# Attention and two dense stages on one core: PSUM banks as tiles of their own, and another order of products, copies and conversions

## The chip, the cores and the metric

The kernel runs on one core of a Trainium2 chip. The metric is the device time of one execution in microseconds (us), less is better. Five engines work side by side, each through its own queue in program order: TensorE (PE; PEld is its loading of weights), VectorE (DVE), ScalarE (ACT), GpSimd (POOL) and SyncE (SP), which here issues most of the DMAs. Results of TensorE land in PSUM, eight banks of 512 fp32 per partition; ACT and DVE read them there.

## The reference

The outputs of an attention with a soft cap (2 x 12 heads, 448 positions, head size 64) form 896 rows of 768, which go through two dense stages, 768 to 2048 to 768 each, the first with h * cos(h), the second with Silu:

```python
scores = cap * np.tanh(scale * np.matmul(q, k.transpose(0, 1, 3, 2)) / cap)
attn = np.exp(scores - np.max(scores, axis=-1, keepdims=True))
x = np.matmul(attn / (np.sum(attn, axis=-1, keepdims=True) + 1e-09), v)
x = np.ascontiguousarray(x.transpose(0, 2, 1, 3)).reshape(B * S, H * D)
h = x @ w_in1;  x = (h * np.cos(h)) @ w_out1
h = x @ w_in2;  return (h * (1.0 / (1.0 + np.exp(-h)))) @ w_out2
```

## The kernel before

Each fp32 operand is split into a high and a low part, and a product is made of three passes of matmuls: high with high, high with low, low with high. The weights come as 64-bit numbers: `w_load` brings a block (two buffers, `wraw`), `w_abs` (ACT) and the three steps of `w_bits` (DVE) turn it into fp32, `w_hi` (ACT) and `w_lo` (DVE) split it into two of the tiles of `room`. The program order of every engine is written out by hand (`manual_schedule`): an engine does its instructions in the order in which the code emits them, and waits where one is not ready.

The stages are attention, `gemm_in` (first weight of the first stage, with cos), `gemm_out` (second weight; result y), `gemm_sums` (first weight of the second stage, with Silu) and `gemm_last` (its second weight). `mm3` (L472) holds the matmuls of `gemm_in` and `gemm_out`, `prod` (L725) those of `gemm_sums`, L898 is `gemm_last`.

`gemm_out` makes six column blocks dm of y^T, each for the two batches b of 448 columns, in three cuts of k. Each block and batch is a sum in one bank. Cut n of block dm also converts the weight that is three cuts ahead, then, in block 5, the first pair of weights of `gemm_sums` (`first_pair`). `gemm_sums` multiplies blocks of 2 x 2 with seven products in place of eight (the scheme of Strassen and Winograd). Its right sides come from y: B11, T1 from blocks 0 to 2 (`y_low`), and B21, B22, T2, T3, T4 from blocks 3 to 5 (`y_high`), each with a high and a low part (`split_hi` on ACT, `split_lo` on DVE). `kept["f"]` is a scratch tile of two halves.

`gemm_sums` runs over eight pairs p of weight blocks. The left sides of a pair are A, S31, S24 and A22; `s31` and `s24` (DVE) form the sums, `take` (ACT) the high and `low` (DVE) the low parts, for the pair q = p + 1 while p is multiplied. A product is nine matmuls of 448 columns. M1 and M5 start a bank, the others add to one: M1, M6, M7 and M4 to `A[p % 3]`, M5 and M3 to `C[p % 2]`, M2 to `Bk[p % 2]`, to which `seed` (ACT) first copies M1. In between, `copy` (ACT) saves the state of a bank (m5, u2), `add` (DVE) adds such a copy to a bank, and `silu` (ACT) makes the outputs. Before, the eight banks are four tiles `ps0` to `ps3` of two banks each; A is banks 0, 1 and 4, C is 2 and 5, Bk is 3 and 7, bank 2n and 2n + 1 being the halves of tile n. All of M4(p) and M7(p) are done in the next pair p + 1.

The last pair (p = 7) also converts the first weights of `gemm_last` (`last_w`) and splits the Silu outputs 0, 1, 8 and 9 (`g_split`). `gemm_last` runs over two halves of the output columns; in each, eight steps p of seven row tiles t, each tile a sum in one bank, six matmuls of 384 columns per step and tile. After a half, ACT and DVE copy the seven sums out and SP writes them.

Of the kernel before, what the change touches and what calls it, by code (L numbers as in the profile page):

```python
# [37 lines left out]
def tile_attention_ffn_ffn(  # L38
# [384 lines left out]

    gpool = ctx.enter_context(tc.tile_pool(name="g", bufs=1, reuse_waits="tile"))
    tpool = ctx.enter_context(tc.tile_pool(name="t", bufs=1, reuse_waits="tile"))
    ps = ctx.enter_context(tc.tile_pool(name="ps", bufs=1, space=PSUM, reuse_waits="tile"))
    ND, GL = 4, 12
    doubles += [(gpool, f"gd{n}") for n in range(ND)]
    halves += [(gpool, f"gh{n}") for n in range(2 * (GL - ND))]
# [28 lines left out]
    def ps_tile():  # L458
        count["ps"] += 1
        return pbank[(count["ps"] - 1) % 4]  # L460
# [103 lines left out]
    def operand(what, j):  # L564
        T[what, j] = Part(f"{what}_{j}")
        return T[what, j].view()
# [7 lines left out]
    def y_low(pt, j, b):  # L574
# [6 lines left out]
        else:  # L581
# [5 lines left out]
            split_hi(t, k[:, 1])  # L587
            split_lo(t, k[:, 1])

    def y_high(pt, j):  # L590
        f, k = kept["f"].view(), kept[j].view()
        t2, t4, t3 = (operand(x, j) for x in ("T2", "T4", "T3"))
        nc.vector.tensor_tensor(out=f[:, 0], in0=pt[1], in1=k[:, 1], op=ALU.add)
        split_hi(t2, f[:, 0])
        nc.vector.tensor_tensor(out=f[:, 1], in0=pt[0], in1=f[:, 0], op=ALU.subtract)
        split_lo(t2, f[:, 0])
        nc.vector.scalar_tensor_tensor(out=f[:, 0], in0=pt[1], scalar=-1.0, in1=k[:, 0], op0=ALU.mult, op1=ALU.subtract)
        kept[j].drop()
        b22 = operand("B22", j)
        split_hi(b22, pt[1])  # L600
        split_hi(t3, f[:, 0])
        split_hi(t4, f[:, 1])
        split_lo(b22, pt[1])
        split_lo(t3, f[:, 0])
        split_lo(t4, f[:, 1])

    def gemm_out(base):
        nxt = base + 3
        held = None
        kept["f"] = Part("f", F32)  # L610
        for dm in range(KD):
            pt = [ps_tile()[:, 0, :S] for b in range(B)]
            for n, (k0, k1) in enumerate(cuts):
                w_load(nxt + 1)
                wi = base + len(cuts) * dm + n
                last = n == len(cuts) - 1
                for b in range(B):
                    mm3(pt[b], wi, gr(k0, k1, b), n == 0, last)
                    if last and dm >= HK and b == 0:
                        t = operand("B21", dm - HK)  # L620
                        split_hi(t, pt[0])
                        split_lo(t, pt[0])
                    if b == 0:
                        if nxt < base_s:
                            for step in range(3):
                                w_bits(nxt, step)
                            w_hi(nxt)
                            w_lo(nxt)
                        else:
                            first_pair(nxt - base_s)  # L630
                        nxt += 1
                        if nxt < base_s + 2:
                            w_abs(nxt)
                    if last and dm < HK:
                        y_low(pt[b], dm, b)
                w_done(wi)
                if dm == KD - 1:
                    for fc in range(k0, k1):
                        drop_g(fc)
                    if n == 0:  # L640
                        w_half(0, 1)
                        w_load(nxt + 1)
                        extend()
                        y_high(held, HK - 2)
            if dm == HK:
                y_high(pt, 0)
            held = pt
        y_high(held, HK - 1)
        kept["f"].drop()

    blocks, whole, xw = {}, {}, {0: wx}

# [6 lines left out]
            room.extend(t[:, e * n:(e + 1) * n].rearrange("p (k f) -> p k f", f=P) for e in range(2))  # L659
        w_abs(base_s + 2, xw[1][:, 0])  # L660

    def w_half(p, jj):
        i = base_s + 2 * p + jj
        if i in w32 or i in wraw:
            w_abs(i, xw[p % 2][:, jj])
            for step in range(3):
                w_bits(i, step)
            del w32[i]

    def s31(p):  # L670
        x = xw[p % 2].bitcast(F32)
# [29 lines left out]
    def first_pair(n):  # L701
        if n == 0:
            w_half(0, 0)
        elif n == 1:
            s31(0)
            take(0, "A")
            low(0, "A")
            take(0, "S31")
            s24(0)
            low(0, "S31")  # L710
        else:
            take(0, "S24")
            low(0, "S24")
            take(0, "A22")
            low(0, "A22")
            w_half(1, 0)

    def prod(bank, p, what, at, rhs, first):
        h, l = blocks[p, what]
# [9 lines left out]

    gf = {}  # L730

    def gemm_sums():
        bank = [t[:, x, :S] for t in pbank for x in range(2)]
        A = [bank[x] for x in (0, 1, 4)]
        C = [bank[x] for x in (2, 5)]
        Bk = [bank[x] for x in (3, 7)]
        u2, m5 = ([t[:, x] for x in range(2)] for t in (Part(f"m{n}", F32).view() for n in range(2)))

        def silu(fc, b, src):
# [40 lines left out]

        def abs_pair(p):
            if p < HP:
                for jj in range(2):
                    w_abs(base_s + 2 * p + jj, xw[p % 2][:, jj])

        for p in range(HP - 1):
            q = p + 1
            M1(p)
            if p:
                add(p - 1, C[(p - 1) % 2], u2[(p - 1) % 2])  # L790
                silu(p - 1, 1, None)
            seed(p)
            w_load(base_s + 2 * q + 1)
            w_half(q, 0)
            w_load(base_s + 2 * q + 2)
            M5(p)
            copy(m5[p % 2], C[p % 2])
            w_half(q, 1)
            w_load(base_s + 2 * q + 3)
            if p:  # L800
                M7(p - 1)
                add(p - 1 + HP, A[(p - 1) % 3], m5[(p - 1) % 2])
            take(q, "A")
            if p:
                silu(p - 1 + HP, 1, None)
            s31(q)
            M2(p)
            low(q, "A")
            silu(p, 0, Bk[p % 2])
            take(q, "S31")  # L810
            M6(p)
            s24(q)
            copy(u2[p % 2], A[p % 3])
            low(q, "S31")
            take(q, "S24")
            low(q, "S24")
            if p:
                M4(p - 1)
                silu(p - 1 + HP, 0, A[(p - 1) % 3])
            take(q, "A22")  # L820
            low(q, "A22")
            abs_pair(q + 1)
            M3(p)
        p = HP - 1
        M1(p)
        add(p - 1, C[(p - 1) % 2], u2[(p - 1) % 2])
        silu(p - 1, 1, None)
        seed(p)
        last_w(0)
        M5(p)  # L830
        copy(m5[p % 2], C[p % 2])
        M7(p - 1)
        add(p - 1 + HP, A[(p - 1) % 3], m5[(p - 1) % 2])
        silu(p - 1 + HP, 1, None)
        g_split(0)
        M6(p)
        copy(u2[p % 2], A[p % 3])
        M4(p - 1)
        silu(p - 1 + HP, 0, A[(p - 1) % 3])
        last_w(1)  # L840
        M2(p)
        silu(p, 0, Bk[p % 2])
        M7(p)
        add(p + HP, A[p % 3], m5[p % 2])
        silu(p + HP, 1, None)
        M3(p)
        add(p, C[p % 2], u2[p % 2])
        silu(p, 1, None)
        g_split(1)
        last_w(2)  # L850
        M4(p)
        silu(p + HP, 0, A[p % 3])

    gs = {}

    def g_split(p):
        if p >= HP:
            return
        if p == 0:
            doubles.extend((gpool, f"gd{n}") for n in range(2))  # L860
        for fc in (p, p + HP):
            if p == 0:
                t = Part(f"gs{fc}", F32R, doubles)
                gs[fc] = (t.view(0), t.view(1))
            else:
                gs[fc] = tuple(Part(f"gs{x}{fc}").view() for x in "hl")
            r = gf[fc].view()
            nc.scalar.activation(out=gs[fc][0], in_=r, func=AF.Copy)
            nc.vector.tensor_tensor(out=gs[fc][1], in0=r, in1=gs[fc][0].bitcast(F32), op=ALU.subtract)
            gf[fc].drop()  # L870

    def last_w(n):
        i = base_l + n
        if i >= len(wjobs):
            return
        w_load(i)
        w_load(i + 1)
        for step in range(3):
            w_bits(i, step)
        w_hi(i)  # L880
        w_lo(i)
        w_abs(i + 1)

    def gemm_last():
        banks = [pbank[n // 2][:, n % 2, :DH] for n in (4, 2, 3, 6, 0, 7, 5, 1)]
        nt = B * S // P
        n = 3
        for half in range(DM // DH):
            pt = [banks[(half * nt + t) % 8] for t in range(nt)]
            for p in range(HP):  # L890
# [6 lines left out]
                        for m, (a, r) in enumerate(((h, wh), (h, wl), (l, wh))):  # L897
                            nc.tensor.matmul(pt[t], a, r[:, cols], start=p == 0 and x == 0 and m == 0, stop=p == HP - 1 and x == 1 and m == 2)  # L898
                w_done(wi)
                if half == 0:  # L900
                    g_split(p + 2)
                last_w(n)
                n += 1
            spare = []
            for t in range(nt):
                if not spare:
# [18 lines left out]
                else:  # L925
                    nc.vector.tensor_copy(o, pt[t])
                nc.sync.dma_start(out[rows, at:at + DH], o)

    gemm_in(0, cos_unit, finish)
    gemm_out(KF)  # L930
    gemm_sums()
    gemm_last()


# [45 lines left out]
```

## Time and profile before

| | us |
|---|---|
| median of 3 runs | 584.09 (583.38 to 1106.0) |
| profiled execution, its own time | 584.23 |
| its span, first to last instruction | 582.5 |
| PE busy in the span | 551.9 (95%) |
| DVE busy | 406.4 (70%) |
| ACT busy | 309.7 (53%) |

Attention takes the first 93.6 us of the profiled execution, `gemm_in` goes to about 210, `gemm_out` to 327.36, `gemm_sums` to 453.36, and `gemm_last` ends at 576.4; what follows are the last copies and writes. Busy times are sums over the span; whether a wait matters is seen only in the stage where it lies. The number in brackets at a line of the timeline is the idle time of the engine before it, with the instruction that ended it. Matmuls overlap in the pipeline, so the drawn end of one lies behind the start of the next.

### The profile page before, as it was taken

What the parts mean: (1) busy time and instruction counts of PE and PEld (TensorE: products, weight loads), DVE (VectorE), ACT (ScalarE), POOL (GpSimd) and SP (SyncE); (2) the same over time, 40 slices, a digit from 0 to 9 for tenths busy, and PEclk for the clock granted to TensorE, in tenths of its full rate; (3) what the DMA queues carried; (4) which work ended last, traced back from release to release, by engine and by line L of the source; (5) the groups of instructions that cost most, each with busy time, mean ns of one, the idle gap of its engine ahead of it and who ended that gap; (6) DMA issues with size and microseconds to landing.
All of it is one profiled execution on the core that took longest, in us unless ns stands there. A gap on an engine that the chain in (4) does not pass through costs nothing.

```text
span 582.5 us, 7411 instructions
## 1 busy us (share of the span) xinstructions
PE 551.9 (95%) x2940; PEld 470.3 (81%) x2940; DVE 406.4 (70%) x556; ACT 309.7 (53%) x392; POOL 31.5 (5%) x50
## 2 busy tenths in 40 slices
PE   8999999999999999999999688999997899999995
PEld 5444446999999999999999576978896799989995
DVE  4589986898888887664467967777866777746201
ACT  6989992777777764423233465555545444422101
POOL 0344430000000000000000000000000000000000
PEclk9999999999999999999999999899999899999999
DMA  7146651233333234432334113333333133544002
GB/s 275 53 139 197 193 164 49 82 133 113 109 109 109 90 100 144 141 103 79 87 124 163 54 55 110 108 109 108 109 108 109 54 110 108 163 146 166 1 1 95
DMA packets 17191, 65.13 MB, mean 112 GB/s; under 512 B 3384, under 2 KB 7268, under 8 KB 17156
## 3 DMA queue, kind: packets, MB, share of 16 engines
q1 hardware_dynamic: 14096, 54.94, 29.1%
q0 software_dynamic: 2496, 9.18, 5.0%
q10 hardware_dynamic: 564, 0.54, 0.3%
q8 instruction: 23, 0.38, 0.2%
q14 instruction: 12, 0.10, 0.0%
HBM read 61.74 MB, written 2.80 MB: 111 GB/s over the span
## 4 chain that ended last, share of the span: by engine, by line
PE 84%; DVE 7%; ACT 6%; issue 2%; DMA 1%; DVEq 0%; ACTq 0%
PE ps L472 36%; PE ps L898 19%; PE ps L725 15%; PE po L277 4%; PE sc L243 3%; PE sm L295 2%; PE sc L247 2%; PE po L287 2%; DVE wx L148 1%; ACT e L255 1%; DVE wx L151 1%; DMA wraw<-in_moe_w_in 1%; DVE wraw L146 1%; ACT wx L135 1%; PE warm L350 1%
## 5 line engine op out<-in xcount | busy, mean ns | idle before, releaser
L472 PE MATMUL ps<-x,hl 128*128 128x448 f32 x576 | 117.0, 365 | 0.0
L472 PEld LDWEIGHTS ps<-x,hl 128*128 128x128 f32 x576 | 108.1, 188 | 9.2 <-DVE xs L314 0.7
L472 PE MATMUL ps<-gh,hl 128*128 128x448 f32 x288 | 83.9, 366 | 0.0
L159 ACT ACTIVATE hl<-wx 128x768 fp32r<-128x768 f32 (+1 forms) x44 | 35.7, 812 | 70.0 <-DVE wx L151 67.2
L898 PE MATMUL ps<-hl,gsh 128*128 128x384 f32 x280 | 71.1, 334 | 0.0
L135 ACT ACTIVATE wx<-wraw 128x768 f32<-128x768 f32 (+1 forms) x66 | 57.1, 874 | 13.2 <-DMA wraw<-in_moe_w_out 7.2
L725 PE MATMUL ps<-T,hl 128*128 128x448 f32 x213 | 51.1, 388 | 13.7 <-ACT ps L776 9.2
L151 DVE SCALAR_TENSOR_TENSOR wx<-wraw,wx 128x768 uint32<-128x768 uint32 (+1 forms) x66 | 61.6, 934 | 2.2
L148 DVE SCALAR_TENSOR_TENSOR wx<-wx,wraw 128x768 int32<-128x768 int32 (+1 forms) x66 | 61.5, 932 | 1.6
L725 PEld LDWEIGHTS ps<-T,hl 128*128 128x128 f32 x213 | 41.7, 200 | 20.9 <-ACT ps L776 11.5
L472 PEld LDWEIGHTS ps<-gh,hl 128*128 128x128 f32 x288 | 54.1, 188 | 4.4
L166 DVE TENSOR_TENSOR hl<-wx,hl 128x768 fp32r<-128x768 f32 (+1 forms) x44 | 40.4, 919 | 23.2 <-ACT hl L159 23.1
L472 PE MATMUL ps<-gl,hl 128*128 128x448 f32 x144 | 52.6, 365 | 0.0
L898 PEld LDWEIGHTS ps<-hl,gsh 128*128 128x128 f32 x280 | 50.6, 188 | 0.0
L898 PE MATMUL ps<-hl,gsl 128*128 128x384 f32 x140 | 46.8, 334 | 0.0
L146 DVE TENSOR_SCALAR wraw<-wraw 128x768 int32<-128x768 int32 (+1 forms) x66 | 35.9, 544 | 15.2 <-ACT wx L135 15.2
L255 ACT ACTIVATE e<-sc,scap 128x896 f32<-128x896 f32 (+1 forms) x48 | 40.0, 913 | 6.7 <-PE sc L243 6.7
L261 ACT ACTIVATE e<-e,capt 128x3136 f32<-128x3136 f32 (+2 forms) x13 | 35.2, 2710 | 0.4
L472 PE MATMUL ps<-g,hl 128*128 128x448 f32 x144 | 31.2, 365 | 0.0
L277 PE MATMUL po<-e,vf 128*64 128x448 f32 x144 | 29.4, 540 | 0.6 <-ACT e L261 0.6
L472 PEld LDWEIGHTS ps<-g,hl 128*128 128x128 f32 x144 | 27.0, 188 | 2.2
L472 PEld LDWEIGHTS ps<-gl,hl 128*128 128x128 f32 x144 | 27.0, 188 | 2.2
(107 smaller groups left out, 814.1 us busy)
## 6 DMA issues: line engine op xcount, KB each, us to landing
wraw<-in_moe_w_in SPq DMA_DIRECT2D x29, 768.0 KB, 4.3
wraw<-in_moe_w_out SPq DMA_DIRECT2D x22, 768.0 KB, 4.3
wraw<-in_moe_w_out SPq DMA_DIRECT2D x12, 640.0 KB, 4.2
raw<-in_qkv POOLq DMA_DIRECT2D x9, 480.0 KB, 4.5
out<-os SPq DMA_DIRECT2D x13, 192.0 KB, 2.1
rb<-rs SPq DMA_DIRECT2D x22, 112.0 KB, 3.2
wraw<-in_moe_w_in POOLq DMA_DIRECT2D x3, 768.0 KB, 5.6
vf<-in_qkv POOLq DMA_DIRECT2D x10, 224.0 KB, 4.7
```

The costliest lines, as they stand in the source:

```text
L135: nc.scalar.activation(out=w32[i][:, :n, :].bitcast(F32), in_=wraw[i][:, :n, :, 1].bitcast(F32), func=AF.Abs, scale=2.0 ** -112)
L146: nc.vector.tensor_scalar(out=w1, in0=w1, scalar1=-0x80000000, scalar2=None, op0=ALU.bitwise_and)
L148: nc.vector.scalar_tensor_tensor(out=t, in0=t, scalar=3, in1=w1, op0=ALU.logical_shift_left, op1=ALU.bitwise_or)
L151: nc.vector.scalar_tensor_tensor(out=t, in0=w0.bitcast(U32), scalar=29, in1=t, op0=ALU.logical_shift_right, op1=ALU.bitwise_or)
L159: nc.scalar.activation(out=whi[i][:, :n, :], in_=w32[i][:, :n, :].bitcast(F32), func=AF.Copy)
L166: nc.vector.tensor_tensor(out=wlo[i][:, :n, :], in0=w32.pop(i)[:, :n, :].bitcast(F32), in1=whi[i][:, :n, :].bitcast(F32), op=ALU.subtract)
L255: nc.scalar.activation(out=e32[p][:, 2 * t:2 * t + n, :], in_=sc.pop((p, t))[:, :n, :S], func=AF.Tanh, scale=scap)
L261: nc.scalar.activation(out=e, in_=e, func=AF.Exp, scale=capt)
L277: nc.tensor.matmul(po[u * D:(u + 1) * D], vf[p][:, 2 * t + u, :], e32[p][:, 2 * t + u, :], start=first and n == 0, stop=last and n == len( ...
L472: nc.tensor.matmul(pt, l, r, start=first and m == 0, stop=last and m == len(ops) - 1)
L725: nc.tensor.matmul(bank, x, y, start=first and m == 0, stop=m == len(ops) - 1, skip_group_check=True)
L898: nc.tensor.matmul(pt[t], a, r[:, cols], start=p == 0 and x == 0 and m == 0, stop=p == HP - 1 and x == 1 and m == 2)
```

## The change

From `gemm_out` on, each PSUM bank is a tile of its own (`bank`, in a new pool that takes the place of the old one); banks are dealt out anew. In `gemm_out`, blocks 3 to 5 do batch 1 ahead of batch 0; `y_high` is split into `y_sums`, `y_high` (both need batch 1 alone) and the three steps of `y_last` (batch 0), and the last block's `y_last` moves into `gemm_sums`, around M1(0). `w_half(1, 0)` moves from `first_pair` into `gemm_sums` too, in two pieces. A Silu on the spent tile `capt` is put into block 1. In `gemm_sums` the work on the next pair's weights becomes a generator, `weights`, whose pieces are dealt out between the products; pair 0 does M7 itself at its end, and the order of the products, of `add`, `silu`, `last_w` and `g_split` in the last pair is another. In `gemm_last`, `last_w` can be done in two parts, and the one of step 7 of half 0 goes behind the copies out. The core of the diff:

```diff
-    ps = ctx.enter_context(tc.tile_pool(name="ps", bufs=1, space=PSUM, reuse_waits="tile"))
+    ps_ctx = ctx.enter_context(ExitStack())
+    ps = ps_ctx.enter_context(tc.tile_pool(name="ps", bufs=1, space=PSUM, reuse_waits="tile"))
...
+    def y_sums(pt, j):
+        f, k = kept["f"].view(), kept[j].view()
+        nc.vector.tensor_tensor(out=f[:, 0], in0=pt, in1=k[:, 1], op=ALU.add)
+        nc.vector.scalar_tensor_tensor(out=f[:, 1], in0=pt, scalar=-1.0, in1=k[:, 0], op0=ALU.mult, op1=ALU.subtract)
+
     def y_high(pt, j):
...
+        f = kept["f"].view()
+        t2, t3 = (operand(x, j) for x in ("T2", "T3"))
         split_hi(t2, f[:, 0])
         split_lo(t2, f[:, 0])
         kept[j].drop()
         b22 = operand("B22", j)
+        split_hi(b22, pt)
+        split_hi(t3, f[:, 1])
+        split_lo(b22, pt)
+        split_lo(t3, f[:, 1])
+
+    def y_last(pt, j, step):
+        f = kept["f"].view()
+        if step == 0:
+            split_hi(operand("B21", j), pt)
+        elif step == 1:
+            split_lo(T["B21", j].view(), pt)
+            nc.vector.tensor_tensor(out=f[:, 1], in0=pt, in1=f[:, 0], op=ALU.subtract)
+            split_hi(operand("T4", j), f[:, 1])
+        else:
+            split_lo(T["T4", j].view(), f[:, 1])
...
-            pt = [ps_tile()[:, 0, :S] for b in range(B)]
+            pt = [bank[(B * dm + b) % 8][:, :S] for b in range(B)]
+            order = (0, 1) if dm < HK else (1, 0)
...
+                for x, b in enumerate(order):
                     mm3(pt[b], wi, gr(k0, k1, b), n == 0, last)
+                    if x == 0 and nxt >= base_s:
+                        first_pair(nxt - base_s)
+                    if last and dm >= HK and x == 0 and dm != KD - 2:
+                        y_sums(pt[1], dm - HK)
+                        y_high(pt[1], dm - HK)
...
+                if dm == 1 and n == 0:
+                    nc.scalar.activation(out=capt, in_=capt, func=AF.Silu)
...
                     if n == 0:
+                        y_sums(held[1], HK - 2)
                         w_half(0, 1)
                         w_load(nxt + 1)
+                        y_high(held[1], HK - 2)
+                        for step in range(3):
+                            y_last(held[0], HK - 2, step)
                         extend()
-                        y_high(held, HK - 2)
...
-        A = [bank[x] for x in (0, 1, 4)]
-        C = [bank[x] for x in (2, 5)]
-        Bk = [bank[x] for x in (3, 7)]
+        A, C, Bk = ([bank[x][:, :S] for x in xs] for xs in ((4, 5, 0), (6, 2), (7, 3)))
...
+        def weights(q):
             w_load(base_s + 2 * q + 1)
             w_half(q, 0)
             w_load(base_s + 2 * q + 2)
+            w_abs(base_s + 2 * q + 1, xw[q % 2][:, 1])
+            yield
             w_half(q, 1)
             w_load(base_s + 2 * q + 3)
+            yield
             take(q, "A")
             s31(q)
+            yield
             low(q, "A")
             take(q, "S31")
+            yield
             s24(q)
             low(q, "S31")
+            yield
             take(q, "S24")
             low(q, "S24")
+            yield
             take(q, "A22")
             low(q, "A22")
             abs_pair(q + 1)
+            yield
...
+        w_half(1, 0, (0,))
+        y_last(pt0, HK - 1, 0)
+        m1(0)
+        y_last(pt0, HK - 1, 1)
+        w_half(1, 0, (1, 2))
+        y_last(pt0, HK - 1, 2)
+        kept["f"].drop()
+        w = weights(1)
+        next(w)
+        m5_(0)
+        next(w)
+        m2(0)
+        next(w)
+        m6(0)
+        next(w)
+        next(w)
+        m3(0)
+        c12(0)
+        m7(0)
+        next(w)
+        next(w)
+        for p in range(1, HP - 1):
+            w = weights(p + 1)
+            m1(p)
+            if p > 1:
+                c12(p - 1)
+            next(w)
+            m5_(p)
+            next(w)
+            if p > 1:
+                m7(p - 1)
+            else:
+                m4(0)
+            next(w)
+            m2(p)
+            next(w)
+            m6(p)
+            next(w)
+            next(w)
+            if p > 1:
+                m4(p - 1)
+            next(w)
+            m3(p)
         p = HP - 1
...
+        last_w(0, 0)
+        m1(p)
+        c12(p - 1)
+        m5_(p)
+        last_w(0, 1)
+        m7(p - 1)
+        m2(p)
+        g_split(0, (0,))
+        last_w(1, 0)
+        m6(p)
+        g_split(0, (1,))
+        m4(p - 1)
+        m7(p)
         g_split(1)
+        m3(p)
+        last_w(1, 1)
+        c12(p)
+        m4(p)
         last_w(2)
...
-        banks = [pbank[n // 2][:, n % 2, :DH] for n in (4, 2, 3, 6, 0, 7, 5, 1)]
+        banks = [bank[n][:, :DH] for n in (0, 1, 6, 7, 4, 3, 2, 5)]
...
+            if half == 0:
+                w_abs(base_l + n)
+            last_w(n)
+            n += 1
...
+    ps_ctx.close()
+    bpool = ctx.enter_context(tc.tile_pool(name="banks", bufs=1, space=PSUM, reuse_waits="tile"))
+    bank = [bpool.tile([P, 512], F32, name=f"bank{n}") for n in range(8)]
+    gemm_sums(gemm_out(KF))
     gemm_last()
```

Here `m1` is M1 and its seed, `m5_` M5 and its copy, `m7` M7 with its `add` and `silu`, `m2`, `m4` a product and its `silu`, `m6` M6 and its copy, `c12` the `add` and `silu` after M3.

## Rows read from the trace of the kernel before

**Rows 1.** The page's first part: busy time, share of the span, instructions.
```profile
PE 551.9 (95%) x2940; PEld 470.3 (81%) x2940; DVE 406.4 (70%) x556; ACT 309.7 (53%) x392; POOL 31.5 (5%) x50
```

**Rows 2.** Waits of PE: who waited for whom, us in total, times, longest us.
```profile
PE ps L725 <- ACT ps L776: 9.2, 6, 5.0
PE ps L725 <- ACT m L776: 3.5, 5, 1.0
PE ps L725 <- DVE gf L748: 3.2, 2, 2.8
PE ps L898 <- ACT gf L743: 2.8, 1, 2.8
PE ps L898 <- ACT os L924: 1.3, 1, 1.3
...
PE ps L725 <- ACT gf L743: 0.6, 1, 0.6
```

**Rows 3.** The chain that ended last, in order of time: start us, us, what.
```profile
93.60 211.35 PE ps L472 x1041
...
517.80 57.55 PE ps L898 x330
```

**Rows 4.** Windows: length, busy us (instructions) of each engine; PEclk, DMA share, GB/s last.
```profile
327.36:346.00 18.64, 12.66 (x53) 10.66 (x52) 12.77 (x19) 8.50 (x14) 0.00 (x0) 0.91 0.27 84
346.00:364.00 18.00, 14.56 (x68) 12.09 (x67) 14.35 (x20) 11.03 (x19) 0.00 (x0) 1.00 0.27 89
364.00:382.00 18.00, 17.37 (x77) 15.41 (x77) 14.39 (x20) 9.32 (x15) 0.00 (x0) 0.91 0.32 102
...
408.32:421.97 13.65, 13.04 (x63) 11.75 (x63) 11.17 (x16) 8.01 (x13) 0.00 (x0) 1.00 0.35 116
...
453.36:476.00 22.64, 19.80 (x105) 19.48 (x104) 16.73 (x19) 11.30 (x15) 0.00 (x0) 0.92 0.31 95
```

**Rows 5.** Timeline of PE, 300 to 461 us: start us, us, instruction, [idle before].
```profile
327.36 1.99 PE L725 MATMUL ps<-B,hl 128*128 128x448 f32 x9
334.36 3.55 PE L725 MATMUL ps<-T,hl 128*128 128x448 f32 x9 [5.01 <-ACT ps L776]
...
346.48 1.99 PE L725 MATMUL ps<-T,hl 128*128 128x448 f32 x9
349.10 2.13 PE L725 MATMUL ps<-T,hl 128*128 128x448 f32 x9 [0.63 <-ACT ps L776]
...
441.41 2.09 PE L725 MATMUL ps<-T,hl 128*128 128x448 f32 x9 [2.75 <-DVE gf L748]
...
460.55 4.74 PE L898 MATMUL ps<-hlx,gs 128*128 128x384 f32 x17 [2.84 <-ACT gf L743]
```

**Rows 6.** Timeline of ACT, 322 to 366 us.
```profile
333.78 0.53 ACT L776 ACTIVATE ps<-ps 128x448 f32<-128x448 f32 x1
...
340.37 1.28 ACT L743 ACT_TABLE_LOAD   x1
```

**Rows 7.** Groups by line, 364 to 435 us, DVE and ACT: busy us, mean ns of one.
```profile
L151 DVE SCALAR_TENSOR_TENSOR wx<-wraw,wx 128x768 uint32<-128x768 uint32 x10 | 9.6, 958 | 0.3
...
L696 DVE TENSOR_TENSOR hl<-sums,hl 128x768 fp32r<-128x768 f32 x7 | 6.7, 954 | 1.3 <-ACT hl L692 1.3
L748 DVE TENSOR_TENSOR gf<-ps,m 128x448 f32<-128x448 f32 x10 | 6.3, 625 | 7.5 <-PE ps L725 7.5
...
L692 ACT ACTIVATE hl<-sums 128x768 fp32r<-128x768 f32 x7 | 5.9, 838 | 0.0
```

**Rows 8.** The page's DMA issues: count, KB each, median us to landing.
```profile
wraw<-in_moe_w_in SPq DMA_DIRECT2D x29, 768.0 KB, 4.3
```

**Rows 9.** Timeline at the two changes of stage, near 93 and 215 us.
```profile
93.53 3.71 PE L472 MATMUL ps<-x,hl 128*128 128x448 f32 x17
93.64 0.62 DVE L309 COPY xu<-po 128x448 f32<-128x448 f32 x1 [0.45 <-PE po L277]
...
215.28 1.09 DVE L519 SCALAR_TENSOR_TENSOR r<-r,ps 128x896 f32<-128x896 f32 x1
```

More of the change, by code (lines that the diff above doesn't have):

```diff
@@ L616, in gemm_out @@
                 last = n == len(cuts) - 1
-                for b in range(B):
+                for x, b in enumerate(order):
                     mm3(pt[b], wi, gr(k0, k1, b), n == 0, last)
[L619 to L623, printed above, removed]
+                    if x == 0 and nxt >= base_s:
[3 more added lines that the diff above has]
+                        y_high(pt[1], dm - HK)
+                    if x == 0:
                         if nxt < base_s:
@@ L640, in gemm_out @@
                     if n == 0:
+                        y_sums(held[1], HK - 2)
                         w_half(0, 1)
                         w_load(nxt + 1)
+                        y_high(held[1], HK - 2)
+                        for step in range(3):
+                            y_last(held[0], HK - 2, step)
                         extend()
-                        y_high(held, HK - 2)
-            if dm == HK:
-                y_high(pt, 0)
+            if HK <= dm < KD - 2:
+                for step in range(3):
+                    y_last(pt[0], dm - HK, step)
             held = pt
-        y_high(held, HK - 1)
-        kept["f"].drop()
+        return pt[0]
     blocks, whole, xw = {}, {}, {0: wx}
@@ L660, in extend, with w_half @@
         w_abs(base_s + 2, xw[1][:, 0])
-    def w_half(p, jj):
+    def w_half(p, jj, steps=range(3)):
         i = base_s + 2 * p + jj
@@ L665, in w_half @@
             w_abs(i, xw[p % 2][:, jj])
-            for step in range(3):
+            for step in steps:
                 w_bits(i, step)
-            del w32[i]
+            if step == 2:
+                del w32[i]
     def s31(p):
@@ L730, in tile_attention_ffn_ffn, with gemm_sums @@
     gf = {}
-    def gemm_sums():
-        bank = [t[:, x, :S] for t in pbank for x in range(2)]
-        A = [bank[x] for x in (0, 1, 4)]
-        C = [bank[x] for x in (2, 5)]
-        Bk = [bank[x] for x in (3, 7)]
+    def gemm_sums(pt0):
+        A, C, Bk = ([bank[x][:, :S] for x in xs] for xs in ((4, 5, 0), (6, 2), (7, 3)))
         u2, m5 = ([t[:, x] for x in range(2)] for t in (Part(f"m{n}", F32).view() for n in range(2)))
@@ L782, in abs_pair @@
             if p < HP:
[L783 to L792, printed above, removed]
+                w_abs(base_s + 2 * p, xw[p % 2][:, 0])
+        def weights(q):
             w_load(base_s + 2 * q + 1)
@@ L822, in gemm_sums @@
             abs_pair(q + 1)
-            M3(p)
-        p = HP - 1
[L825 to L848, printed above, removed]
+            yield
+        def m1(p):
+            M1(p)
+            seed(p)
+        def m5_(p):
+            M5(p)
+            copy(m5[p % 2], C[p % 2])
+        def m7(p):
+            M7(p)
+            add(p + HP, A[p % 3], m5[p % 2])
+            silu(p + HP, 1, None)
+        def m2(p):
+            M2(p)
+            silu(p, 0, Bk[p % 2])
@@ new lines, in m6, with m4, m3, c12 @@
+        def m6(p):
+            M6(p)
+            copy(u2[p % 2], A[p % 3])
+        def m4(p):
+            M4(p)
+            silu(p + HP, 0, A[p % 3])
+        def m3(p):
+            M3(p)
+        def c12(p):
+            add(p, C[p % 2], u2[p % 2])
+            silu(p, 1, None)
+        w_half(1, 0, (0,))
[6 more added lines that the diff above has]
+        w = weights(1)
@@ L849, in gemm_sums, with g_split @@
+        p = HP - 1
+        last_w(0, 0)
[11 more added lines that the diff above has]
+        m7(p)
         g_split(1)
+        m3(p)
+        last_w(1, 1)
+        c12(p)
+        m4(p)
         last_w(2)
-        M4(p)
-        silu(p + HP, 0, A[p % 3])
     gs = {}
-    def g_split(p):
+    def g_split(p, parts=(0, 1)):
         if p >= HP:
@@ L858, in g_split @@
             return
-        if p == 0:
+        if p == 0 and 0 in parts:
             doubles.extend((gpool, f"gd{n}") for n in range(2))
-        for fc in (p, p + HP):
+        for fc in (p + HP * n for n in parts):
             if p == 0:
@@ L870, in g_split, with last_w @@
             gf[fc].drop()
-    def last_w(n):
+    def last_w(n, part=None):
         i = base_l + n
@@ L875, in last_w @@
             return
[L876 to L882, printed above, removed]
+        if part != 1:
+            w_load(i)
+            w_load(i + 1)
+            for step in range(3):
+                w_bits(i, step)
+        if part != 0:
+            w_hi(i)
+            w_lo(i)
+            if n != HP + 2:
+                w_abs(i + 1)
     def gemm_last():
-        banks = [pbank[n // 2][:, n % 2, :DH] for n in (4, 2, 3, 6, 0, 7, 5, 1)]
+        banks = [bank[n][:, :DH] for n in (0, 1, 6, 7, 4, 3, 2, 5)]
         nt = B * S // P
@@ L899, in gemm_last @@
                 w_done(wi)
[L900 to L903, printed above, removed]
+                if p < HP - 1:
+                    early_g = p < 2
+                    if half == 0 and early_g:
+                        g_split(p + 2)
+                    last_w(n, 0)
+                    if half == 0 and not early_g:
+                        g_split(p + 2)
+                    last_w(n, 1)
+                    n += 1
             spare = []
@@ L927, in gemm_last @@
                 nc.sync.dma_start(out[rows, at:at + DH], o)
+            if half == 0:
+                w_abs(base_l + n)
+            last_w(n)
+            n += 1
     gemm_in(0, cos_unit, finish)
-    gemm_out(KF)
-    gemm_sums()
+    ps_ctx.close()
+    bpool = ctx.enter_context(tc.tile_pool(name="banks", bufs=1, space=PSUM, reuse_waits="tile"))
+    bank = [bpool.tile([P, 512], F32, name=f"bank{n}") for n in range(8)]
+    gemm_sums(gemm_out(KF))
     gemm_last()
```

29 lines of the change are left out of this document (removed).

## The prediction, made before the result was known

> **What bounds the kernel now.** I read the page first: TensorE (PE) is busy for 95% of the span [rows 1]. So either its matmuls get cheaper or its pauses go, and the change alters no matmul. Next the waits of PE, grouped by who was waited for [rows 2]. All of these groups stand in lines 725 (the products of the pairs, `prod`) and 898 (`gemm_last`): 9.2 + 3.5 + 3.2 + 2.8 + 1.3 + 0.6 = 20.6 us in 16 waits. The chain of waits then shows that PE has no pause from 93.60 on for 211.35 us, 1041 matmuls at 0.203 us each [rows 3]; everything to be won lies behind that, from the last part of `gemm_out` on. The windows show two things there [rows 4]: the granted clock is 0.91, 0.91 and 0.92 in three stretches, and a pair of the middle (408.32 to 421.97) takes 13.65 us for its 63 matmuls, which at 0.203 need 12.8.
>
> The timeline of PE names the waits [rows 5]. M1(0) starts at 327.36, M5(0) only at 334.36, after 5.01 us of waiting. Its releaser is the `seed` copy on ScalarE (ACT), which ran at 333.78 [rows 6] because it stood in ACT's queue behind the copies of `y_high(held, 2)`. M5(0) does not read what `seed(0)` writes: M5 writes bank 2, the seed writes bank 3. They are two halves of one tile, `ps1`. The same at 349.10: M7(0) writes bank 0 and waits for `seed(1)`, which reads bank 1, the other half of `ps0`. M5(1), in between at 346.48, writes bank 5 of `ps2`, has no tile in common with `seed(1)`, and does not wait for it. At 441.41 M6(7) (bank 1) waits for an addition that reads bank 0; at 460.55 the last stage's bank 0 waits for the last Silu, which reads bank 1. So the waits go by tile, not by bank, and the pairs of banks are laid out such that neighbouring steps meet in one tile.
>
> **What the change does, and the sum.**
> *Waits removed.* Eight tiles of one bank. I went through the banks of the new order, A = 4, 5, 0, C = 6, 2, Bk = 7, 3 (and of the last stage 0, 1, 6, 7, 4, 3, 2, 5): no product writes a bank whose last reader is the step just before it. The true dependences that are left (the u2 copy before M7, the seed before M2, the m5 copy before M3, the `add` before M4) each have at least one product of nine matmuls, 1.83 us, in between. Terms: the 20.6 us of waits [rows 2]. Each restart costs a little more than its wait, since a matmul is drawn 0.36 us long but the next one starts 0.203 us later when nothing is waited for: 16 x 0.16 = 2.6 us. The clock: (1 - 0.91) x 18.64 + (1 - 0.91) x 18.00 + (1 - 0.92) x 22.64 = 1.7 + 1.6 + 1.8 = 5.1 us [rows 4]; each fall follows or sits on one of the long pauses (5.01 us; the crowd of pauses of 346 to 364, 14.56 busy of 18.00; 2.84 us), so it goes with them. Sum 28.3 us.
> *Cross-check from counts.* From 327.36 to the end of the last matmul at 517.80 + 57.55 + 1.0 for the six matmuls of the last tile, 576.4, are 249.0 us. In them are 504 matmuls of the pairs (504 x 0.203 = 102.3) and 672 of the last stage (57.55 / 330 = 0.1744 each, 117.2) [rows 3, 5]: 219.5. The difference is 29.5 us. The two ways give 28.3 and 29.5; I take 28.9.
>
> *Moved: the first pair.* T2, B22 and T3 of the last column block are now made from b = 1 while PE does the 15 matmuls of b = 0 (3.05 us). VectorE (DVE) has five operations of some 0.63 us for them (an operation of 448 columns that reads a bank [rows 7]), so it is done about 0.4 us after M1(0) starts; the moved `w_half(1, 0)`, two operations of 0.96 [rows 7] and a shorter one, some 2.5 us, no longer stands ahead of them. B21 and T4 come after. M2(0), the first product that needs one, starts after two products, 3.66 us: B21's low part is there at 0.4 + 0.55 + 0.63 = 1.6, the seed at 1.83 + 0.2 + 0.53 = 2.6. If these covers failed PE would wait again for a part of the 5.01 us.
> *DVE in the first three pairs* is where the new order is tightest, as PE now comes earlier. M5(2) is the fourteenth product and starts 13 x 1.83 = 23.8 us after M1(0). Ahead of it DVE must have done: 0.4 of backlog, three y operations (1.9), and what it does for pairs 1 and 2, 2 x 11.17 (the middle pair [rows 4]), less what of pair 2 comes later, the low parts of S24 and of the half as wide A22 (0.95 + 0.5) and two additions (1.2): 22.0 us. By the order of the queues it also waits some 1.4 us for ACT's high parts (0.84 us each [rows 7]). That is 23.4 against 23.8: no wait, by 0.4 us. The same margin, 0.4, comes out for M4(1), which waits for `add(9)`. From there on a pair takes DVE 11.17 us and ACT 8.01 [rows 4] against 12.8 of PE, so the margin grows by 1.6 a pair. The bit steps' loads land 4.3 us after issue [rows 8]; each is issued a half pair or more (6 us) before its `w_abs`.
> *The last pair.* Nine products, 16.5 us, then the last stage. M4(7), ninth, waits for `add(15)`. DVE's queue up to it: two weights' bit steps, a low part, three additions, two low parts of g of some 1.0 us (896 columns; twice the 0.63 of 448 would be the most), with waits for M7(6) and for ACT; walked through it ends 13.8 us after M1(7), M4(7) starts at 14.6. gs(0), gs(8) and weight 50 are ready at 13.3 against 16.5; the last Silu reads bank 5, which the first half does not use.
> *The rest costs nothing.* The Silu on `capt` in `gemm_out` brings its table load, 1.28 us now at 340.37 [rows 6], into a stretch where PE has three cuts of weights ahead; without that cover ACT would be 1.28 us late for `y_low`. Swapping b in `gemm_out` and putting y's work ahead of a weight's bits delays that weight by 3 us out of the 19.5 us (96 matmuls) until its use. The last `last_w` of half 0 goes behind the copies out; its weight is used two steps (14.6 us) later.
> *Added waits.* For the three tight places I allow one wait of the size seen now, 0.62 + 0.16 = 0.8 us. The profiled execution took 584.23 us (span 582.5 and 1.7 around it), 0.14 over the median of 584.09. 584.2 - 28.9 + 0.8 = 556.1.
>
> *A rule against it.* In the stretch 408.32 to 421.97, with a wait of 0.62 us in it, the clock stayed at 1.00 [rows 4]; only pauses of 2.8 us and more, or crowded ones, came with a fall. The Trainium skill (TensorE: Matmul & The Clock Gate, "A second HAM failure mode: psum-queue depth-cycling") says that groups which go round PSUM banks, with short pauses between them, can make the clock swing between its two levels. By it a new order that keeps short pauses would keep the falls too; rival 2 is that case, priced from rows.
>
> **Rivals.**
> 1. *The new pool waits for the whole old one.* The first matmul of `gemm_out` would wait until the last unit of `gemm_in` has read its tile: 93.6 + 576 x 0.203 = 210.5 to 216.4 [rows 9], 5.9 us, with a fall of the clock 1.7: 563.7. Against it: at the change from attention, PE wrote the first new tile at 93.53, before the old `po` began to be read at 93.64 [rows 9].
> 2. *Short waits stay and the clock keeps falling.* One wait of 0.8 us in each of six pairs (4.8), three falls (5.1): 566.0. For it: margins of 0.4 us. Against it: DVE's slack in the middle pairs.
> 3. *The change doesn't do what it says:* the waits have another cause than the shared tile. Then only the three longest go, by the order (5.0, 2.8 and 2.8 [rows 2]), and 13 stay: 10.0 us, 2.1 of restarts, and one fall of the clock, 1.7: 569.1, up to 584 if the long ones stay too. Against it: M5(1) did not wait for `seed(1)`, with which it shares no tile; M7(0) behind it did [rows 5].
> 4. *Slower: DVE and ACT become the bound.* Same work, another order: if each handing over between them were exposed, a pair would follow their chain and not PE. To be back at 584, each of eight pairs must take 28 / 8 = 3.5 us more, 16.3 in all; to be 2% slower (596), 17.8. DVE's 11.17 would need 5 to 6.6 us of waiting a pair; the pair shown now has 13.65 - 11.17 = 2.5. Price 584 to 600, likeliest 596.
>
> **How the numbers follow.** Forecast 0.81; its own range is 554.7 (29.5 gone, nothing new) to 560 (28.3 gone, three waits of 0.8 and a fall of 1.7). Rival 1 0.04, rival 2 0.06, rival 3 0.05, rival 4 0.04. The predicted time is the forecast's, 556. The range reaches down to 553.5 (a rate of matmuls 0.5% better than my 219.5 us) and up to 564, which takes in rival 1. Beyond 2% (11.7 us, about what a measurement here tells from no change): faster is below 572.4, which is the forecast, rivals 1 and 2 and 0.01 of rival 3: 0.92. Within 2%: 0.04 of rival 3 and 0.01 of rival 4: 0.05. Slower: 0.03.
>
> **What would show it.** In the profile after: PE's waits behind 327 us under 3 us in total, none on the seed; M1(0) to M1(7) in 423 x 0.203 = 86 us; the clock at 1.00 to the last matmul; a pair in 12.8 us; no pause at the first matmul of `gemm_out` (else rival 1); DVE's idle time waiting on PE, not PE on DVE (else rival 4). The forecast is wrong if waits of 0.6 us on copies stay in the middle pairs, or if PE waits for DVE's additions in pairs 1 to 3.

## The result

The changed kernel took 551.71 us (551.54 to 551.79), the kernel before 584.87 (583.38 to 585.65, and one run of 1106.0 that the ratio leaves out): a ratio of 0.944 with a 95% interval of 0.942 to 0.946. That is faster, as forecast, but below the range: 556.0 had been forecast, 553.5 to 564. The profiled execution took 551.79 us with a span of 550.0, 1.8 apart (1.7 before).

The page's first part, the answer to [rows 1]; then the waits of PE over the whole execution, the answer to [rows 2]; then the chain that ended last from the end of attention on, the answer to [rows 3].

```profile
PE 542.1 (99%) x2940; PEld 467.2 (85%) x2940; DVE 404.9 (74%) x556; ACT 309.0 (56%) x393; POOL 31.1 (6%) x50
```

```profile
PE warm L350 <- DVE zero L361: 1.4, 1, 1.4
PE sm L295 <- DVE e L303: 0.9, 1, 0.9
PE po L277 <- ACT e L261: 0.7, 1, 0.7
PE sc L247 <- ACT e L255: 0.6, 1, 0.6
PE po L287 <- ACT e L261: 0.2, 1, 0.2
```

```profile
93.36 116.94 PE ps L473 x576
210.29 116.99 PE bank L473 x576
327.29 102.15 PE bank L741 x504
429.44 116.50 PE bank L967 x672
```

The reader is to see in the waits that nothing of [rows 2] is left: all five lie ahead of 93.3 us, in attention and its start. In the chain the four stages of 576, 576, 504 and 672 matmuls stand end to end without a piece between them (L473 is `mm3`, L741 `prod`, L967 the last stage). The windows of the changed kernel, with the columns of [rows 4]:

```profile
327.29:429.44 102.15, 102.15 (x505) 94.65 (x505) 88.55 (x120) 63.51 (x105) 0.00 (x0) 1.00 0.37 124
392.00:404.80 12.80, 12.80 (x65) 11.86 (x64) 11.20 (x16) 7.71 (x13) 0.00 (x0) 1.00 0.37 122
```

PE is busy all of the time and the clock is at 1.00; in the length of a pair, 12.8 us, DVE works 11.2. Where the 32.5 us of span went: from the first product to the end of the last matmul it is 327.36 to 576.37 before and 327.12 to 545.93 after, 249.0 against 218.8, so 30.2; the stretch behind the last matmul shrank from 6.1 to 4.1, 2.0; the first product came 0.24 earlier.

The copies out at the end, which the prediction did not look at, by the timeline of ACT and SP; first before, then after (seven row tiles; ACT copies the even ones):

```profile
575.37 0.87 ACT L924 ACTIVATE os<-ps 128x384 f32<-128x384 f32 x2 [31.37 <-PE ps L898]
575.89 2.81 SPq L927 DMA_DIRECT2D out<-os  x6
...
578.82 0.40 SPq L921 DMA_DIRECT2D out<-os  x1
```

```profile
539.72 0.49 ACT L998 ACTIVATE os<-bank 128x384 f32<-128x384 f32 x1 [23.82 <-PE bank L967]
540.24 5.60 SPq L1001 DMA_DIRECT2D out<-os  x6
...
546.71 0.33 SPq L995 DMA_DIRECT2D out<-os  x1
```

Before, the copy of the first row tile (bank 1) started at 575.37, five row tiles after its own matmuls were done: the sixth (bank 0) goes into the other half of `ps0`. All writes to memory queued behind it. After, it starts 6.2 us before the last matmul ends, and the last write is issued 0.8 us behind that end (545.93) in place of 2.45 (576.37).

### The profile page after: what moved, and what is told of

It is laid out like the page before. It is cut to its first block, busy times and chain, and to the rows that moved or that the text cites. A ratio compares the mean times of both kernels' runs of the same rounds, so it can differ in the third digit from the quotient of the medians.

```text
span 550.0 us, 7421 instructions
## 1 busy us (share of the span) xinstructions
PE 542.1 (99%) x2940; PEld 467.2 (85%) x2940; DVE 404.9 (74%) x556; ACT 309.0 (56%) x393; POOL 31.1 (6%) x50
## 4 chain that ended last, share of the span: by engine, by line
PE 95%; ACT 2%; issue 1%; DMA 1%; DVE 1%
PE bank L473 21%; PE ps L473 21%; PE bank L967 21%; PE bank L741 19%; PE po L277 5%; PE sc L243 3%; PE sm L295 2%; PE sc L247 2%; PE po L287 2%; ACT e L255 1%; DMA raw<-in_qkv 1%; ACT e L261 1%; DVE e L303 0%; DVE ql L227 0%; DVE qh L226 0%
## 5 line engine op out<-in xcount | busy, mean ns | idle before, releaser
L473 PE MATMUL ps<-x,hl 128*128 128x448 f32 x576 | 117.0, 365 | 0.0
L473 PEld LDWEIGHTS ps<-x,hl 128*128 128x128 f32 x576 | 108.1, 188 | 9.2 <-DVE xs L314 0.7
L473 PE MATMUL bank<-gh,hl 128*128 128x448 f32 x288 | 83.9, 366 | 0.0
L967 PE MATMUL bank<-hl,gsh 128*128 128x384 f32 x280 | 71.0, 334 | 0.0
L473 PEld LDWEIGHTS bank<-gh,hl 128*128 128x128 f32 x288 | 54.1, 188 | 4.4
L473 PE MATMUL bank<-gl,hl 128*128 128x448 f32 x144 | 52.6, 365 | 0.0
L967 PEld LDWEIGHTS bank<-hl,gsh 128*128 128x128 f32 x280 | 50.5, 188 | 0.0
L741 PE MATMUL bank<-T,hl 128*128 128x448 f32 x234 | 50.2, 365 | 0.0
L741 PEld LDWEIGHTS bank<-T,hl 128*128 128x128 f32 x234 | 43.9, 188 | 3.5
L967 PE MATMUL bank<-hl,gsl 128*128 128x384 f32 x140 | 46.8, 334 | 0.0
L473 PE MATMUL bank<-g,hl 128*128 128x448 f32 x144 | 31.2, 365 | 0.0
L473 PEld LDWEIGHTS bank<-g,hl 128*128 128x128 f32 x144 | 27.1, 188 | 2.2
```

Source lines behind the costliest of these rows:

```text
L473: nc.tensor.matmul(pt, l, r, start=first and m == 0, stop=last and m == len(ops) - 1)
L741: nc.tensor.matmul(bank, x, y, start=first and m == 0, stop=m == len(ops) - 1, skip_group_check=True)
```

## The experiments

**What tiles and order are worth alone.** Theory: a wait goes to every reader and writer of the same tile, whichever bank; so the eight tiles carry the gain, and the order settles what is left at the two ends. The rival: the order carries it.

The tiles alone: the kernel before, with

```diff
+    ps_ctx.close()
+    bpool = ctx.enter_context(tc.tile_pool(name="banks", bufs=1, space=PSUM, reuse_waits="tile"))
+    bank8 = [bpool.tile([P, 512], F32, name=f"bank{n}") for n in range(8)]
...
-            pt = [ps_tile()[:, 0, :S] for b in range(B)]
+            pt = [bank8[2 * ((B * dm + b) % 4)][:, :S] for b in range(B)]
...
-        bank = [t[:, x, :S] for t in pbank for x in range(2)]
+        bank = [t[:, :S] for t in bank8]
...
-        banks = [pbank[n // 2][:, n % 2, :DH] for n in (4, 2, 3, 6, 0, 7, 5, 1)]
+        banks = [bank8[n][:, :DH] for n in (4, 2, 3, 6, 0, 7, 5, 1)]
```

> The order of before, but from gemm_out on each bank is a tile of its own; the banks are those of before. Theory (the tile makes the waits, the order matters only at the two ends): the waits of the middle pairs, of the last stage and of the final copies go. What stays is real: M2(0) needs seed(0), which stands in ACT's queue until about 334.3, so PE waits about 3.3 us there; M4(6) waits about 0.9 us for an addition; perhaps a clock fall of 1.7. 556 to 559 us, last matmul to end of span 4.0 us (6.1 before). Rival (the new order carries the gain by putting products between a copy and the next write of its tile): 570 us or more.

Measured: 559.65 us, ratio 0.960 (0.957 to 0.963). Its waits of PE outside attention:

```profile
PE bank L726 <- ACT bank L777: 3.0, 1, 3.0
PE bank L726 <- DVE gf L749: 1.8, 2, 1.0
```

The theory holds: 13 of the 16 waits are gone with no operation moved. The 3.0 us are M2(0) behind `seed(0)`, a true dependence, as expected to 0.3 us; the 1.8 are two additions of the last pair. The span is 9.0 us longer than with the change. By the starts of its matmuls that is 4.8 of waits, 0.8 of restarts, 1.5 of a fall of the clock after the 3.0 (granted clock 0.66 from 334 to 339), and about 1.7 that nobody had expected (below).

The order alone: the changed kernel with its banks put back as halves of four tiles.

```diff
-    bank = [bpool.tile([P, 512], F32, name=f"bank{n}") for n in range(8)]
+    two = [bpool.tile([P, B, 512], F32, name=f"two{n}") for n in range(4)]
+    bank = [two[n // 2][:, n % 2, :] for n in range(8)]
```

> The changed kernel with its eight banks put back as halves of four tiles; order and bank numbers of the change. Theory (waits go by tile): M5 waits for the seed in each pair, as C and Bk meet in one tile, and M4(p-1) for the u2 copy where A's banks 4 and 5 meet: some nine waits of 0.8 us, and the final copies wait as before (2 us): 559 to 564 us. Rival (the order alone has the gain): 554 or less. Rival (the tiles alone have it): 575 or more.

Measured: 585.25 us, no gain. The waits of PE show why this was not the experiment meant:

```profile
PE two L473 <- DVE B L573: 13.6, 5, 5.0
PE two L741 <- ACT two L789: 5.2, 8, 0.9
PE two L741 <- ACT m L789: 2.0, 3, 0.7
```

The 13.6 us are in `gemm_out`: the change puts the sums of both batches into neighbouring banks, which here share a tile. The kernel before avoids that by using only the first half of each tile there. The next two kernels do the same.

```diff
-            pt = [bank[(B * dm + b) % 8][:, :S] for b in range(B)]
+            pt = [bank[2 * (2, 3, 1, 0)[(B * dm + b) % 4]][:, :S] for b in range(B)]
```

> As order_only, but in gemm_out the two batches of a block get banks in different tiles, as they have before and after the change. In order_only they shared one, and PE waited 13.6 us there and lost 3.4 to the clock, which is no part of the question. Theory (waits go by tile; order and tiles share the gain): the waits order_only had in gemm_sums stay, 8.5 us in 13 waits, with restarts of 2.1 and the slow tail of 2.1: 564 to 566 us. Rival (the order has no worth without the tiles): 575 or more.

Measured: 571.35 us, between the two forecasts. The cause was the second batch of the first block of `gemm_out`, on a tile that `gemm_in` was still reading, in the timeline of PE:

```profile
216.39 3.73 PE L473 MATMUL two<-g,hl 128*128 128x448 f32 x12 [2.33 <-DVE r L520]
```

That is 2.3 us of waiting, with a fall of the clock behind it (0.66 from 217 to 222, 1.7 us), and the mechanism of rival 1 on one tile. So once more, with the blocks dealt out past it:

```diff
+            pt = [bank[2 * n][:, :S] for n in ((0, 1), (2, 3), (0, 3), (1, 2), (2, 3), (1, 0))[dm]]
```

> The order of the change on four tiles of two banks, with the sums of gemm_out dealt out so that none of them meets a tile still being read: order_fair put the first block on the tile that gemm_in read last, and PE waited 2.3 us there and lost 1.7 to the clock. Theory: those 4.1 us go, the 13 waits of gemm_sums and the slow tail stay: 567 us. Rival (something else of the order costs time on shared tiles): 570 or more.

Measured: 566.6 us, ratio 0.970 (0.968 to 0.972), against an expected 567. The window over all of `gemm_sums`:

```profile
327.30:441.90 114.60, 106.11 (x505) 93.62 (x504) 90.27 (x121) 64.49 (x105) 0.00 (x0) 1.00 0.34 110
```

So each part alone is worth a good deal: the tiles 24 us, the order 17, both together 33. Eight or so of the 33 are had by either: the two waits of 2.8 us go with one as with the other, and the one of 5.0 shrinks to 3.0 with the tiles and goes with the order. What this order leaves and the tiles remove are 13 waits of 0.6 to 0.9 us, and the slow tail (6.3 us behind the last matmul with the order alone, 3.8 with the tiles alone).

**The tail by itself.** The kernel before with one line changed:

```diff
-        banks = [pbank[n // 2][:, n % 2, :DH] for n in (4, 2, 3, 6, 0, 7, 5, 1)]
+        banks = [pbank[n // 2][:, n % 2, :DH] for n in (3, 6, 7, 4, 5, 0, 1, 2)]
```

> The kernel before with one line changed: the order of the banks in gemm_last, chosen so that the two halves of a tile are used by neighbouring row tiles. Theory (the final copies waited for matmuls into the other half of their tile): the stretch from the last matmul to the end of the span falls from 6.1 to about 4.1 us, the wait of 1.3 at the start of the second half goes, that of 2.8 at the start of the stage shrinks by 1.0: 579 to 580, or 578 if the fall of the clock at 460 goes too. Rival (the shorter tail of the changed kernel comes from the moved last_w, or from the writes): tail stays at 6.1, 581 to 582.5.

Measured: 577.35 us, ratio 0.990 (0.988 to 0.993), a little less than expected. The last matmul ends at 572.2, the span at 576.2: 4.0 us, as in the changed kernel. Timeline of ACT:

```profile
567.01 0.49 ACT L924 ACTIVATE os<-ps 128x384 f32<-128x384 f32 x1 [28.74 <-PE ps L898]
569.11 0.49 ACT L924 ACTIVATE os<-ps 128x384 f32<-128x384 f32 x1 [1.60 <-PE ps L898]
571.20 0.49 ACT L924 ACTIVATE os<-ps 128x384 f32<-128x384 f32 x1 [1.60 <-PE ps L898]
```

Each copy now waits for one more row tile only, the one in the other half. Neither the moved `last_w` nor the new tiles are in this kernel, so the cause of the slow tail is which row tiles share a tile; eight tiles remove it, and so does another dealing out of the four. Of the 6.2 us of span that it gains, 2.0 are the tail and 2.6 the last stage's two waits, as expected; the other 1.6 lie ahead of that line (the clock fell at other places, the first product came 0.45 earlier), where nothing was edited. The fall of the clock at the start of the last stage did not go.

**The last row tile in one copy.** The changed kernel without

```diff
-                if t == nt - 1 and half == 1:
-                    c = DH // 2
-                    nc.scalar.activation(out=o[:, :c], in_=pt[t][:, :c], func=AF.Copy)
-                    nc.vector.tensor_copy(o[:, c:], pt[t][:, c:])
...
```

> The changed kernel with the last row tile copied by ACT alone and written by one DMA, like the others. In the profile of the changed kernel DVE's half of that copy waits for ACT's half, as both read one bank: 0.33 + 0.36 and a write each. One copy takes 0.49: 0.2 us less, if the one write of 192 KB lands as fast as the two of 96: 551.5. Rival (the longer write takes the gain back): 551.7 or a little more.

Measured: 551.65 us, the same. The last matmul ends at 545.63 and the span at 549.7, 4.1 us behind it as before. The larger write takes back what the copy saves: a write of 192 KB lands 1.9 us after its issue (median of seven), the two of 96 KB took 1.7 and 1.6. The difference between the medians, 0.06 us, is within the scatter of the runs.

**The table load.** The changed kernel without the Silu on `capt`.

```diff
-                if dm == 1 and n == 0:
-                    nc.scalar.activation(out=capt, in_=capt, func=AF.Silu)
```

> The changed kernel without the Silu on the spent tile in gemm_out, so that the table load falls on the first real Silu, after M2(0). Theory (hidden either way, but for the narrow margin): 1.28 us later on ACT, 0.6 us later for DVE's low part of A(1), against a margin of 0.4 us at M5(2): 551.7 to 552.3. Rival (the preload is part of the gain): the load holds up the copy of u2(0) and M7(0) behind it: 553 or more.

Measured: 552.02 us (551.71 to 552.08), 0.3 more. In the profile the load stands at 331.83 for 1.28 us, beside M2(0), and `gemm_sums` still takes 102.15 us for its 504 matmuls, without a wait. That part of the change hides nothing that was seen; the 0.3 us by which this span is longer lie ahead of `gemm_sums`.

**How near DVE is to the limit.** The changed kernel with the subtraction of s31 done twice, and four times, for each pair (1 and 3 more):

```diff
             take(q, "A")
-            s31(q)
+            for _ in range(2):
+                s31(q)
```

> The changed kernel with the subtraction of s31 done twice for each of the pairs 1 to 7 (the same values again): 0.87 us more of DVE per pair. Theory (PE sets the pace; DVE has 1.6 us to spare per pair, but only 0.4 us up to M5(2)): PE waits 1.3 to 1.7 us around pairs 2 and 3 and nowhere later: 553 to 553.6. Rival (DVE, already at the limit, sets the pace): 0.87 x 7 = 6.1, 557 to 558. Rival (the margins are wider than drawn): 551.7.

> The same with s31 done four times: 2.6 us more of DVE per pair, 13.8 against 12.8 of PE. Theory: 4.8 us of waiting by M5(2), then about 1.0 a pair for five pairs: 560 to 563. Rival (DVE sets the pace already): 2.6 x 7 = 18, 570.

Measured: 554.79 us and 566.91 us. First the waits of PE for one more, then for three more, then the window of 60 us in the middle for the change itself and for both:

```profile
PE bank L741 <- DVE hlx L713: 0.8, 1, 0.8
...
PE bank L741 <- DVE gf L761: 0.2, 1, 0.2
```

```profile
PE bank L741 <- DVE hlx L713: 4.6, 4, 3.4
PE bank L741 <- DVE gf L761: 3.0, 6, 1.0
```

```profile
365.00:425.00 60.00, 60.00 (x297) 55.60 (x297) 50.78 (x68) 36.68 (x61) 0.00 (x0) 1.00 0.36 119
```

```profile
365.00:425.00 60.00, 60.00 (x292) 54.51 (x291) 53.39 (x73) 37.33 (x62) 0.00 (x0) 1.00 0.36 119
```

```profile
365.00:425.00 60.00, 57.50 (x274) 50.34 (x272) 58.37 (x77) 32.13 (x55) 0.00 (x0) 1.00 0.35 117
```

With one more, PE waits twice, at 349.1 and 359.2, and nowhere later, as the theory had it; the starts of its matmuls show 1.63 us lost there. With three more, DVE sets the pace: 58.4 of 60 us busy, and a pair takes 14.16 us (392.54 to 406.70). That is 11.17 + 3 x 1.0: a repeated subtraction starts only when the one before has ended (four of them take 3.93 us), so it costs 1.0 and not 0.87, some 0.4 us a pair. That is part of why 566.9 came out and not 560 to 563; a fall of the clock behind the wait of 3.4 us (0.66 from 354.8 to 359.8, 1.7 us) is another, and the rest was not followed up. But one more cost 3.1 us, not 1.6. The windows show the rest: 292 matmuls in 60 busy us, where the change has 297.

**A pause alone.** To part the slower matmuls from DVE's extra work, the same subtraction was done four times for pair 2 only:

```diff
+            for _ in range(4 if q == 2 else 1):
+                s31(q)
```

> The changed kernel with the subtraction of s31 done four times for pair 2 alone: 2.6 us more of DVE once, nothing in any other pair. In the profile of dve1 the matmuls after its second wait follow each other at 207 ns in place of 203, up to the last stage, though PE waited 1.0 us in all. Theory A (a pause can leave PE at the slower spacing until the next one): one or two waits, 2.2 us by the margin of 0.4, and the spacing afterwards at 207 (1.4 to 1.7 us more in all: 555.4) or at 203 (554). Theory B (the slower spacing came from DVE's extra work beside PE): 203 from pair 3 on, 554.

Measured: 555.12 us (554.75 to 556.98). In the profiled execution, PE waited 1.9 and 0.2 us, and from the second wait on the same window reads:

```profile
365.00:425.00 60.00, 60.00 (x298) 55.60 (x297) 50.77 (x70) 37.87 (x64) 0.00 (x0) 1.00 0.36 119
```

So here the matmuls were back at the faster spacing. Between the two waits they were not: from 354 to 360.6 their starts lie 207 ns apart, though the last of the extra subtractions had ended at 350.8. What lies behind the second wait speaks for neither side. The window of the tiles alone speaks for the pause; that kernel has no extra work on DVE, less of it than the change even, and one pause of 3.0 us before it:

```profile
365.00:425.00 60.00, 60.00 (x292) 54.51 (x291) 48.73 (x66) 35.26 (x58) 0.00 (x0) 1.00 0.31 105
```

292 again, and the starts show the same spacing from 338, where the clock was back, to the next wait at 427. DVE's extra work is not needed for it, and with three more subtractions a pair the matmuls between waits ran at 203 ns from 359 to 434.

## Why the prediction was right in its cause and wrong in its size

**Right: the mechanism.** The waits went by tile, all 16 went, and with them the falls of the clock. No short wait came in their place. The order of the queues was walked through closely enough: M5(2) was said to start 0.4 us after DVE had its operand, and DVE's operation ends at 350.42 with M5(2) at 350.84; M4(7) was put 14.6 us after M1(7) and came after 14.6, with `add(15)` 0.6 ahead of it (0.8 forecast). That a pair has 1.6 us of DVE to spare is what the runs with more work on DVE showed, to the 0.4 us at its start.

**Wrong: the step "waits removed" counted only PE's waits.** It was made from "who PE waited for" [rows 2], as if a shared tile held up only the engine that writes it. It holds up readers as well: the copies out waited for matmuls into the other half, and PE, being done, could not show it. The sum kept the 6.1 us behind the last matmul; they became 4.1. That is 2.0 us, the largest single part of the miss, and the kernel with only the last stage's banks changed shows it apart from the rest. It took this and the terms below together to leave the range: 556.1 - 2.0 = 554.1 is still inside it.

**Mis-sized: the cross-check from counts.** 57.55 / 330 = 0.1744 us per matmul of the last stage includes the drawn end of the last one and the slow first ones behind a wait. Their spacing is 116.50 / 672 = 0.1734, 0.7 us less over the stage. With it the count gives 30.2 us, which is what was measured; the sum of waits, restarts and clock gave 28.3. The mean of the two, 28.9, cost another 0.6 against the count's own 29.5. What the sum of waits lacks lies mostly in its restarts: they were priced at 0.16 us from how long a matmul is drawn, but nine matmuls behind a wait also take 2.09 us where nine others take 1.99 (441.41 and 346.48 in [rows 5]), so 16 restarts cost some 16 x 0.1 = 1.6 us more. A smaller part, some 0.7 us by the starts, is the slower spacing after some pauses, which it did not know.

**Not needed: the allowance** of one wait, 0.8 us. In all 556.1 - 2.0 - 0.7 - 0.6 - 0.8 = 552.0, and 0.24 us of an earlier first product.

**The rivals.** The new pool did not wait for the old one: the chain has `gemm_out` follow `gemm_in` at 210.29 with nothing between. Short waits did not stay. The third rival, another cause than the tile, falls with the kernel in which only the tiles differ. DVE did not become the bound; by its 11.2 us in 12.8 it would with some 1.6 us more per pair, and with 3 more it was. The range itself was too narrow below, because every unknown that it took in was a cost: it left 1.2 us for gains that had not been thought of.

**The rule on short pauses.** Rival 2 did not come, as no short wait was left. In the kernel with the order alone, `gemm_sums` keeps 13 waits of 0.6 to 0.9 us, and its window above shows the clock at 1.00 throughout. The Trainium skill (TensorE: Matmul & The Clock Gate, "A second HAM failure mode: psum-queue depth-cycling") has the clock swing in a kernel with short pauses between groups; in this window the measurement does not agree with it. Nor did the forecast's own reading hold, that only pauses of 2.8 us and more, or crowded ones, come with a fall: the single one of 2.3 us above did.

## What to carry to other kernels

Where a framework keeps track of a tile as a whole, a tile of two banks is one lock: give each bank that is filled and emptied on its own a tile of its own, which here was worth 24 of 584 us without moving an instruction. When the cost of such a lock is added up, look at both sides of it, at the writers that wait and at the readers that start late, and above all at the end of the program, where no later wait shows the loss. With a tile for each bank, what an order by hand still had to cover here were true dependences (4.8 us of waits with the tiles alone); walk each queue to its tightest point and keep the margin as a number, since a later edit of 1 us may use it up.

## What the runs showed of the hardware

Matmuls of 448 columns follow each other in one of two rhythms, 203 or 207 ns on average, at the same granted clock of 1.00. In the products of `gemm_sums` the rhythm changed only at a pause of PE (the shortest of 0.1 us) and then held until another pause or the next shape: 292 matmuls in 60 us against 297. With the tiles alone the slower one held from 338 to 427 us, with one more subtraction a pair from 352 to the last stage, through the wait at 359.2; that is some 1.6 us each. After other pauses it stayed at or returned to 203. It means that a single short wait can cost more than its length.

A pause is not needed for it, though. In `gemm_out` of the kernels before and after the change, where PE never waits, the last 15 or so matmuls of each of the six blocks run at 207 ns, and what follows the block goes back to 203. The timeline of PE before the change, near the end of block 4, has starts 0.60 us apart for three matmuls, then 0.62, and 2.44 for twelve in the block that follows:

```profile
304.57 0.56 PE L472 MATMUL ps<-gh,hl 128*128 128x448 f32 x2
305.17 0.58 PE L472 MATMUL ps<-gh,hl 128*128 128x448 f32 x2
305.79 0.58 PE L472 MATMUL ps<-gh,hl 128*128 128x448 f32 x2
...
307.86 2.60 PE L472 MATMUL ps<-g,hl 128*128 128x448 f32 x12
310.30 0.37 PE L472 MATMUL ps<-gh,hl 128*128 128x448 f32 x1
```

What decides the rhythm was not found.

A fall of the clock does not follow from the length of one pause either: a wait of 1.8 us (at 459.0, last stage of the kernel with its banks changed; granted clock 0.66 from 458 to 463) and one of 2.3 us (216.4) were followed by one, waits of 2.7 us (at 439.9 of the same kernel, 1.00 from 436 to 446, and 441.41 in [rows 5]) were not.
